# Accumulators put in banks one group ahead, residual rows loaded at once, first left-over rows split in place

## The chip, the cores and the metric

The kernel runs on one core of one Trainium2 chip. The metric is the device time of one execution in microseconds (us), the median over the runs. The engines are called PE (matrix multiplication, with PEld for its weight loads), DVE (vector), ACT (scalar), POOL and SP; SP does nothing but issue transfers (DMA), which ACT also issues. "Banks" are the eight banks of PSUM, the memory that PE writes its sums to.

## The reference

One transformer block on 2048 rows of 576 features, in fp32: an adaptive layer norm, a segmented linear-memory attention, a residual; then a second adaptive layer norm, a gated feed-forward layer with 4608 hidden features, and a residual.

```python
mod = (_silu(c) @ w_mod).reshape(c.shape[0], 6, 1, -1)
sa, ca, ga, sb, cb, gb = (mod[:, 0], mod[:, 1], mod[:, 2], mod[:, 3], mod[:, 4], mod[:, 5])
h = _layernorm(x) * (1 + ca) + sa
x = x + ga * _A_ref(h, A_wq, A_wk, A_wv, A_wo, A_beta)   # 32 heads, 4 segments of 512 rows, output times wo
h = _layernorm(x) * (1 + cb) + sb
x = x + gb * ((_silu(h @ w_gate) * (h @ w_up)) @ w_down)
```

## The kernel before, in words

**Precision.** Every fp32 operand is split into a high part (a cast to the PE's fp32r format, on ACT) and a low part (value minus high part, on DVE); a product is then three matmuls, high x high, high x low and low x high. Products of 2 x 2 blocks use a seven-product scheme, so operands are sums and differences of blocks as well.

**Up to 523 us.** Layer norm, q, k, v, attention and the output product wo run interleaved, in an order written out by hand. The last stage of it, wo for the last segment (`wo_m`, 32 small blocks n = 0 to 31, products at line 876), runs from 523 to 552 us. In its loop, work for the feed-forward half is placed at fixed n: loads of the operands `y` (`load_y`, four blocks of 1 MB and their remainder), three more operand blocks that are made in place (`y_here`), sums and splits of the first weights (`O` to `wh` and `wl`, `prep_w`).

**Left-over rows.** The 576 features are 4 x 128 + 64, so each seven-product has a seventh matmul over 96 rows, whose weights are three stacked copies (high, low, high) of 32 left-over rows, in two tiles `R` (`wr0`, `wr1`). Left-over rows of four weight blocks at a time come as a tile `RB` (`load_rb`), are summed (`sum_rb`), split (`split_rb`: `RH` on ACT, the low part on DVE), and stored to a DRAM buffer `rD` (`store_rb`), from where `prep_r` loads the wanted 32 rows three times. For the first two tiles `first_r` takes them from `RB` by six transfers on ACT's queue.

**The feed-forward half, from 552 us.** Loops over 2 halves of the tokens (t), 18 blocks of hidden features (p, "passes") and 14 steps (k). A step is one of the seven products of gate or up: seven matmuls of 512 columns at line 1459, into one of the banks A, B or C. ACT copies from these (`tb`, `tc`, B; line 1488 and 1505) feed the sums on DVE that make gate times up. Between the steps stands the down projection of the pass before: in passes 8 to 16 of the first half, 14 groups c = 0 to 13 of six matmuls of 288 columns (line 1589), one per step, two at steps 4 (c = 4 and 5) and 11 (c = 11 and 12), none at steps 6 and 13. The matmuls of a group write a tile `pd` of two banks, of which there are two. For nine of the 14 groups (`PA7`) the running sum `acc` is copied into the tile by ACT ahead of the matmuls (line 1569), and out of it behind them (line 1593); for the others DVE adds the tile to the sum (line 1597). `down` asks for its own and the next group's tile ahead of its matmuls, and for the one after that behind them (`ahead`). In the second half the sums are added on DVE alone. In passes 1 to 7 the down projection has another form (line 1613).

**Operand preparation for the second half.** `prep2` is a generator, advanced at steps of passes 1 to 7: it loads five blocks of 128 rows of the residual stream `xD`, normalises them (statistics on DVE at line 1300, scale on ACT), stores them, and then makes the operands of the second half from them. The rows go through two buffers.

**What sets the order.** Each engine works through its own instructions in the order of the program; waits are semaphores. A tile from a pool is written only when its last readers are done. Transfers use eight semaphores in turn, so a transfer also waits for the one that was issued eight before it. Low parts are put in a list `later` and issued with the next step.

Of the kernel before, what the change touches and what calls it, by code (L numbers as in the profile page):

```python
# [15 lines left out]
P = 128  # L16
S = 2048
D = 576
# [4 lines left out]
L = 512  # L23
# [78 lines left out]
def f32(ap):  # L102
    return ap.bitcast(F32)
# [3 lines left out]
def block(ctx: ExitStack, tc: tile.TileContext, x, wqk, wv, wo, beta, wgu, wrm, wd, c, w_mod, wm01, out):  # L107
# [1154 lines left out]
            later.append(lambda: nc.vector.tensor_tensor(d[64:96], f[64:96], f32(d[64:96]), op=ALU.subtract))  # L1262

    def prep2(x2p):
        ha = xp.tile([P, 2, L], F32, tag="xs", name="ha")
        xb = xp.tile([P, 4, 2, P], F32, tag="xs", name="xb")[:, :, 0]
        t3 = x2p.tile([P, 256], F32, tag="t3", name="t3")

        def opr(kb, hv, o, f):
# [11 lines left out]
            yield  # L1281

        xl2 = x2p.tile([P, D], F32, tag="xl2", name="xl2")
        xls = (ha.rearrange("p a b -> p (a b)")[:, :D], xl2)
        rows = ((2, 3), (3, 0), (3, 1), (3, 2), (3, 3))

        def load_row(j):
            sn, i = rows[j]
            nc.sync.dma_start(xls[j % 2], xD[sn][:, i, :])
        load_row(0)  # L1290
        load_row(1)
        for _ in range(5):
            yield
        for j, (sn, i) in enumerate(rows):
            xl = xls[j % 2]
# [12 lines left out]
            nc.scalar.activation(xl, xl, AF.Identity, scale=rs[:, 0:1], bias=nb[:, 0:1])  # L1308
            nc.sync.dma_start(xhD[sn][:, i, :], xl)
            if j < 3:  # L1310
                load_row(j + 2)
            yield
        xbs = (xb, xl2[:, :L].rearrange("p (a b) -> p a b", b=P))

# [70 lines left out]

    RB = {}

    def load_rb(j):
        RB[j] = opl.tile([P, 7, P], F32, tag="RB", name="RB")
        nc.sync.dma_start(RB[j][:, 0:4], wrm[j])  # L1390

    def sum_rb(j, i):
        sum_w(RB[j], i, nc.gpsimd if j else nc.vector)

    def split_rb(j):
        r = RB[j]
        rh = RB[j, 1] = opl.tile([P, 7, P], F32R, tag="RH", name="RH")
        nc.scalar.copy(rh, r)
        later.append(lambda: nc.vector.tensor_tensor(r.bitcast(F32R), r, f32(rh), op=ALU.subtract))

    def first_r():
        for z in range(2):
            for c in range(3):
                v = RB[0] if c == 1 else f32(RB[0, 1])
                nc.scalar.dma_start(f32(R[z][32 * c:32 * c + 32]), v[32 * z:32 * z + 32])

    def store_rb(j):
        lo, hi = RB.pop(j), f32(RB.pop((j, 1)))
        for c, v in ((0, hi), (2, hi), (1, lo)):
            nc.scalar.dma_start(rD[j][c], v)  # L1410

# [148 lines left out]
    PD = {}  # L1560
# [13 lines left out]
            down_new(t, *v)  # L1574

    def down(t, p, c):
        for j in range(c, c + 2 - t):
            ahead(t, p, j)
        m, q = POS[c // 2], c % 2
        ah, al = AP[p % 2, m]  # L1580
        dh, dl = DP[p % 2, m]
        pd = PD[t, p, c]
        new = p == (0 if t else P7) and m not in (2, 3, 4)
        on_act = t == 0 and c in PA7
        first = new or not on_act
        for i in range(2):
            tk = slice(128 * (2 * q + i), 128 * (2 * q + i) + 128)
            for k, (a, w) in enumerate(((ah, dh), (ah, dl), (al, dh))):
                nc.tensor.matmul(pd[:, i, :288], lhsT=a[:, tk], rhs=w, start=(first and k == 0), stop=(k == 2),  # L1589
                                 skip_group_check=not first)  # L1590
        o = down_acc(t, c)
        if on_act:
            nc.scalar.copy(o, pd[:, :, :288])  # L1593
        elif new:
            nc.vector.tensor_copy(o, pd[:, :, :288])
        else:
            nc.vector.tensor_tensor(o, o, pd[:, :, :288], op=ALU.add)  # L1597
        if t == 0:
            ahead(t, p, c + 2)

    def plain(t, p, c):
        end = t and p == NPR - 1 and c == 7
# [53 lines left out]
    with tc.manual_schedule():  # L1656
# [58 lines left out]
        ys = [hvp.tile([P, L], F32, tag="hh2", name="ys"), yt[2][:, 4, :L],  # L1715
              pool(p5, "ys").tile([P, L], F32, tag="ys", name="ys")]
        load_o(0, 0, 0)
        load_rb(0)
        for kb in range(3):
            y_sum(kb)  # L1720
        load_y(0, 0)
# [14 lines left out]
        for i in range(4):  # L1736
            for h in range(2):
                for c in range(WC):
                    n = 8 * i + 4 * h + c
                    wo_m(3, i, h, c)  # L1740
                    if c == 3:
                        wo_x(3, i, h)
                    flush()
                    if n in SS:
                        j = SS.index(n)
                        sum_o(0, j // 4, j % 4, nc.vector if j > 3 else nc.gpsimd)
                    if n == 6:
                        for z in range(2):
                            nc.gpsimd.memset(f32(R[z][96:128]), 0.0)
                        for o in ACT_OP.values():  # L1750
                            nc.gpsimd.memset(f32(y[96:128, o, 4]), 0.0)
                    if n == 9:
                        for j in range(4):
                            sum_rb(0, j)
                    elif n == 10:
                        split_rb(0)
                    elif n == 12:
                        first_r()
                    elif n == 28:
                        store_rb(0)  # L1760
                    if n == 24:
                        nc.scalar.activation(omg[:, 0:1], omg[:, 0:1], AF.Silu)
                        store_o(0, 0)
                    if n in HH:
                        y_here(HH.index(n))
                    if n in WW:
                        prep_w(0, 0, next(gw))
                if h == 1 and i < 2:
                    wo_r(3, i + 2)
                    wo_s(3, i + 2)  # L1770
                    wo_t(3, i + 2)
# [21 lines left out]
        for t in range(2):  # L1793
            for p in range(NPR):
# [17 lines left out]
                for k in range(14):  # L1812
# [28 lines left out]
                    else:  # L1841
# [158 lines left out]
```

## Time and profile before

| | us |
|---|---|
| median of 3 runs | 1808.68 (1804.61 to 1812.76) |
| the profiled execution | 1806.46 |
| its span | 1804.7 |
| PE busy | 1762.7 (98%) |
| PE loading weights | 1496.8 (83%) |
| DVE busy | 1473.2 (82%) |
| ACT busy | 1032.2 (57%) |
| POOL busy | 486.2 (27%) |
| last wo stage | 523 to 552 |
| first half of the feed-forward part | 552 to 1178 |
| second half | 1178 to the end |

In rows of the timeline the columns are the start (us), the duration (us), engine, line, operation, output and input tiles, count, and in brackets how long the engine was idle before and what ended that. In rows of groups the numbers behind the bar are busy time, mean ns of one, and the idle time before such instructions with its releaser. In rows of windows, the busy time of each engine stands with its number of instructions, then the granted clock of PE, the busy share of the DMA engines and what they moved in GB/s. Matmuls overlap: a row of 0.29 us is followed by the next after 0.13.

### The profile page before, as it was taken

What the parts mean: (1) busy time and instruction counts of PE and PEld (TensorE: products, weight loads), DVE (VectorE), ACT (ScalarE), POOL (GpSimd) and SP (SyncE); (2) the same over time, 40 slices, a digit from 0 to 9 for tenths busy, and PEclk for the clock granted to TensorE, in tenths of its full rate; (3) what the DMA queues carried; (4) which work ended last, traced back from release to release, by engine and by line L of the source; (5) the groups of instructions that cost most, each with busy time, mean ns of one, the idle gap of its engine ahead of it and who ended that gap; (6) DMA issues with size and microseconds to landing.
All of it is one profiled execution on the core that took longest, in us unless ns stands there. A gap on an engine that the chain in (4) does not pass through costs nothing.

```text
span 1804.7 us, 31494 instructions
## 1 busy us (share of the span) xinstructions
PE 1762.7 (98%) x10945; PEld 1496.8 (83%) x10945; DVE 1473.2 (82%) x3290; ACT 1032.2 (57%) x2221; POOL 486.2 (27%) x748
## 2 busy tenths in 40 slices
PE   8999999999988999999999999999999999999999
PEld 5888777767767888888888888888888888888888
DVE  7567589989966788987888888868888888898886
ACT  6343578778855455545787777444544544544542
POOL 2010146555670555453454444100000000000000
PEclk9999999999999999999999999999999999999999
DMA  8678765577668677644544544594324324324331
GB/s 310 224 234 278 239 200 175 169 198 210 192 216 303 202 240 231 208 153 134 175 137 136 182 141 137 172 302 150 102 85 131 106 81 130 108 80 131 108 104 53
DMA packets 149190, 309.85 MB, mean 172 GB/s; under 512 B 28184, under 2 KB 60376, under 8 KB 147240
## 3 DMA queue, kind: packets, MB, share of 16 engines
q1 hardware_dynamic: 134536, 253.29, 46.0%
q10 hardware_dynamic: 14496, 54.55, 7.7%
q8 instruction: 87, 1.43, 0.3%
q14 instruction: 71, 0.58, 0.1%
HBM read 193.04 MB, written 113.33 MB: 170 GB/s over the span
## 4 chain that ended last, share of the span: by engine, by line
PE 72%; DMA 4%; DVE 4%; ACT 4%; issue 1%; POOL 1%; ACTq 0%; SPq 0%; DVEq 0%; POOLq 0%
PE A L1459 22%; PE pd L1589 14%; PE C L1459 11%; PE pd L1613 6%; PE B L1459 6%; PE pw L876 3%; PE av L768 3%; PE s L713 2%; PE s L742 2%; PE pn L1012 1%; DVE junk L213 1%; ACT acc L1593 1%; DMA O<-in_wgu_dram 1%; DMA y<-yD 1%; DMA wd<-dr__15586 1%
## 5 line engine op out<-in xcount | busy, mean ns | idle before, releaser
L1459 PE MATMUL A<-y,wh 128*128 128x512 f32 x1152 | 404.3, 391 | 3.1 <-ACT tb L1488 2.0
L1459 PEld LDWEIGHTS A<-y,wh 128*128 128x128 f32 x1152 | 216.4, 188 | 43.7 <-ACT tb L1488 3.2
L1597 DVE TENSOR_TENSOR acc<-acc,pd 128x576 f32<-128x576 f32 x258 | 193.7, 751 | 64.6 <-PE pd L1589 58.9
L1424 DVE TENSOR_TENSOR wl<-O,wh 128x256 fp32r<-128x256 f32 x504 | 245.2, 490 | 1.4 <-ACT wh L1423 0.9
L213 DVE CUSTOM_DVE_ANT_0 junk<-s,tri 128x384 bf16<-128x384 f32 (+3 forms) x512 | 218.5, 486 | 22.7 <-PE s L713 8.9
L1459 PE MATMUL A<-y,wl 128*128 128x512 f32 x576 | 224.9, 390 | 0.0
L1589 PE MATMUL pd<-dh,ah 128*128 128x288 f32 x700 | 208.7, 298 | 8.8 <-ACT acc L1593 8.8
L1423 ACT CAST wh<-O 128x256 fp32r<-128x256 f32 x504 | 199.5, 406 | 17.8 <-DMA wr<-RH 9.4
L1589 PE MATMUL pd<-dl,ah 128*128 128x288 f32 x700 | 206.1, 294 | 0.0
L1589 PE MATMUL pd<-dh,al 128*128 128x288 f32 x700 | 205.1, 293 | 0.0
L1459 PE MATMUL C<-y,wh 128*128 128x512 f32 x576 | 202.7, 393 | 0.0
L1529 DVE TENSOR_TENSOR al<-sg,ah 128x512 fp32r<-128x512 f32 x219 | 160.9, 735 | 7.9 <-ACT ah L1528 7.3
L1528 ACT CAST ah<-sg 128x512 fp32r<-128x512 f32 x219 | 135.9, 621 | 52.0 <-DVE sg L1483 43.8
L1589 PEld LDWEIGHTS pd<-dh,ah 128*128 128x128 f32 x700 | 131.4, 188 | 22.5 <-ACT acc L1593 10.6
L1414 POOL TENSOR_TENSOR O<-O 128x256 f32<-128x256 f32 x132 | 114.6, 885 | 124.3 <-DMA O<-in_wgu_dram 57.4
L749 ACT ACTIVATE Pt<-s 128x512 f32<-128x512 f32 x256 | 135.4, 598 | 21.6 <-PE s L742 11.8
L1589 PEld LDWEIGHTS pd<-dl,ah 128*128 128x128 f32 x700 | 132.4, 189 | 13.1
L1589 PEld LDWEIGHTS pd<-dh,al 128*128 128x128 f32 x700 | 132.1, 189 | 0.0
L1459 PEld LDWEIGHTS C<-y,wh 128*128 128x128 f32 x576 | 108.0, 188 | 18.9
L1459 PEld LDWEIGHTS A<-y,wl 128*128 128x128 f32 x576 | 108.1, 188 | 15.4
L1459 PE MATMUL A<-y,wr 128*128 128x512 f32 x288 | 113.8, 395 | 0.0
L1459 PE MATMUL C<-y,wl 128*128 128x512 f32 x288 | 112.2, 389 | 0.0
(422 smaller groups left out, 4305.1 us busy)
## 6 DMA issues: line engine op xcount, KB each, us to landing
wr<-rD SPq DMA_DIRECT2D x207, 112.0 KB
O<-in_wgu_dram SPq DMA_DIRECT2D x36, 512.0 KB
O<-oD SPq DMA_DIRECT2D x36, 512.0 KB
oD<-O ACTq DMA_DIRECT2D x34, 512.0 KB
ks<-kD SPq DMA_DIRECT2D x64, 216.0 KB
qs<-qD SPq DMA_DIRECT2D x64, 216.0 KB
O<-in_wgu_dram SPq DMA_DIRECT2D x36, 384.0 KB
y<-yD SPq DMA_DIRECT2D x11, 1024.0 KB
```

Source lines behind the costliest of these rows:

```text
L213: nc.vector.tensor_tensor_reduce(junk[:, :n], bank[:, o:o + n], tri[:, L - n:], 1.0, -3e38, op0=ALU.add, op1=ALU.max, accum_out=mcol[u][0] ...
L749: nc.scalar.activation(pt[:, h], bank, AF.Exp, scale=SCALE)
L768: nc.tensor.matmul(av[u][32 * h:32 * h + 32, 128 * j:L], lhsT=vq[s][:, j, VW * hh:VW * hh + 32], rhs=pt[:, h, c:c + L - 128 * j], start=(j ...
L1414: eng.tensor_tensor(o[:, d], o[:, a], o[:, b], op=op)
L1423: nc.scalar.copy(wh, o)
L1424: later.append(lambda: nc.vector.tensor_tensor(wl, o, f32(wh), op=ALU.subtract))
L1459: nc.tensor.matmul(bank, lhsT=a, rhs=b, start=(first and n == 0), stop=(n == 6), skip_group_check=not first)
L1528: nc.scalar.copy(ah, src)
L1529: later.append(lambda: nc.vector.tensor_tensor(al, src, f32(ah), op=ALU.subtract))
L1589: nc.tensor.matmul(pd[:, i, :288], lhsT=a[:, tk], rhs=w, start=(first and k == 0), stop=(k == 2), skip_group_check=not first)
L1597: nc.vector.tensor_tensor(o, o, pd[:, :, :288], op=ALU.add)
L1613: nc.tensor.matmul(pd[:, i, :288], lhsT=a[:, tk], rhs=w, start=(k == 0), stop=(k == 5))
```

## The change

There are three parts.

1. `down` asks for its own tile ahead of its matmuls and for the next group's tile behind them, ahead of its own copy-out. Before, it was two groups ahead. Only the first half does so; in the second, `down` asks for its own alone, as before.
2. `prep2` loads all five rows at its start, into halves of two larger tiles and one tile of its own, and has one more turn before the first row is read.
3. The first left-over rows: `load_first` loads the 32 rows three times, straight to the partitions where they are wanted, by six transfers on SP; `sum_first` sums them on DVE, four instructions over 96 partitions and both tiles; `split_first` writes each `R` by one cast on ACT, and the low part in its middle 32 partitions on DVE. The rows of `RB[0]`, wanted from the second pass on, are loaded, summed (on POOL), split and stored in steps 0 to 6 of the first pass. High and low parts now share one tile.

```diff
 def prep2(x2p):
-    ha = xp.tile([P, 2, L], F32, tag="xs", name="ha")
-    xb = xp.tile([P, 4, 2, P], F32, tag="xs", name="xb")[:, :, 0]
+    xa, xc = [xp.tile([P, 4, 288], F32, tag="xs", name=f"x{n}").rearrange("p a b -> p (a b)") for n in "ac"]
+    ha = xa[:, :2 * L].rearrange("p (a b) -> p a b", a=2)
+    xb = xc[:, :L].rearrange("p (a b) -> p a b", b=P)
...
-    xls = (ha.rearrange("p a b -> p (a b)")[:, :D], xl2)
+    xls = (xl2, xc[:, :D], xc[:, D:], xa[:, :D], xa[:, D:])
     rows = ((2, 3), (3, 0), (3, 1), (3, 2), (3, 3))
-    def load_row(j):
-        sn, i = rows[j]
-        nc.sync.dma_start(xls[j % 2], xD[sn][:, i, :])
-    load_row(0)
-    load_row(1)
-    for _ in range(5):
+    for j, (sn, i) in enumerate(rows):
+        nc.sync.dma_start(xls[j], xD[sn][:, i, :])
+    for _ in range(6):
         yield
...
         nc.sync.dma_start(xhD[sn][:, i, :], xl)
-        if j < 3:
-            load_row(j + 2)
         yield
...
-def first_r():
+def load_first():
+    RB["first"] = r = new_rb()
     for z in range(2):
         for c in range(3):
-            v = RB[0] if c == 1 else f32(RB[0, 1])
-            nc.scalar.dma_start(f32(R[z][32 * c:32 * c + 32]), v[32 * z:32 * z + 32])
+            nc.sync.dma_start(r[32 * c:32 * c + 32, z, 0:4], wrm[0][32 * z:32 * z + 32])
+
+def sum_first(i):
+    sum_w(RB["first"][0:96].rearrange("p z a b -> p a z b"), i, nc.vector)
+
+def split_first(z):
+    r = RB["first"][:, z]
+    nc.scalar.copy(R[z][0:96], r[0:96])
+    later.append(lambda: nc.vector.tensor_tensor(R[z][32:64], r[32:64], f32(R[z][32:64]), op=ALU.subtract))
...
 def down(t, p, c):
-    for j in range(c, c + 2 - t):
-        ahead(t, p, j)
+    ahead(t, p, c)
...
+    if t == 0:
+        ahead(t, p, c + 1)
     o = down_acc(t, c)
     if on_act:
         nc.scalar.copy(o, pd[:, :, :288])
...
-    if t == 0:
-        ahead(t, p, c + 2)
...
-    load_rb(0)
+    load_first()
...
                 if n == 9:
                     for j in range(4):
-                        sum_rb(0, j)
-                elif n == 10:
-                    split_rb(0)
-                elif n == 12:
-                    first_r()
-                elif n == 28:
-                    store_rb(0)
+                        sum_first(j)
+                elif n in (11, 14):
+                    split_first(n // 14)
...
+                    elif p == 0 and k < 8:
+                        if k == 0:
+                            load_rb(0)
+                        elif k == 2:
+                            for j in range(4):
+                                sum_rb(0, j)
+                        elif k == 4:
+                            split_rb(0)
+                        elif k == 6:
+                            store_rb(0)
```

What follows are pieces of the engines' own orders. The lines of the changed kernel differ from those of before by a few (1569 is 1574, 1593 is 1599, 1423 is 1428, 1488 is 1493, 1379 is 1374, 1405 is gone).

ACT in the last wo stage, before (`hh` is the cast that the next wo products read, `wh` the high part of a weight block):

```order
L1398 CAST RH_8555<-RB_8436 128x896
L1423 CAST wh_8563<-O_8434 128x256
L1405 DMA wr0_8421<-RH_8555 32x896
L1405 DMA wr0_8421<-RB_8436 32x896
L1405 DMA wr0_8421<-RH_8555 32x896
L1405 DMA wr1_8422<-RH_8555 32x896
L1405 DMA wr1_8422<-RB_8436 32x896
L1405 DMA wr1_8422<-RH_8555 32x896
L1423 CAST wh_8590<-O_8434 128x256
L855 CAST hh_8598<-pto_8593 128x512
```

And now:

```order
L1409 CAST wr0_8421<-RB_8436 96x896
L1428 CAST wh_8566<-O_8434 128x256
L1409 CAST wr1_8422<-RB_8436 96x896
L1428 CAST wh_8590<-O_8434 128x256
L855 CAST hh_8598<-pto_8593 128x512
```

The six transfers ahead of `hh` are gone from ACT, and there are two casts where one was.

SP around the rows of `prep2` (in the first passes), before (`ha` and `xl2` are the two buffers, `xh` the normalised rows in DRAM):

```order
L1289 DMA ha_9000<-xD2_125 128x576
L1289 DMA xl2_9003<-xD3_126 128x576
L1373 DMA O_9019<-in_wgu_dram 128x1024
L1384 DMA wr1_8422<-rD0_181 32x896 x3
L1309 DMA xh2_121<-ha_9000 128x576
L1289 DMA ha_9000<-xD3_126 128x576
L1373 DMA O_9217<-in_wgu_dram 128x1024
L1309 DMA xh3_122<-xl2_9003 128x576
L1289 DMA xl2_9003<-xD3_126 128x576
L1384 DMA wr0_8421<-rD1_182 32x896 x3
L1309 DMA xh3_122<-ha_9000 128x576
L1289 DMA ha_9000<-xD3_126 128x576
```

And now:

```order
L1288 DMA xl2_9011<-xD2_125 128x576
L1288 DMA xc_9009<-xD3_126 128x576 x2
L1288 DMA xa_9008<-xD3_126 128x576 x2
L1368 DMA O_9030<-in_wgu_dram 128x1024
L1379 DMA wr1_8422<-rD0_181 32x896 x3
L1306 DMA xh2_121<-xl2_9011 128x576
L1368 DMA O_9226<-in_wgu_dram 128x1024
L1306 DMA xh3_122<-xc_9009 128x576
```

The three later loads no longer stand behind the stores of earlier rows; all five follow one another.

ACT at steps 10 to 12 of a pass of the first half, before (the tile `pd_12648` is that of group 12, `pd_12592` that of group 10; `tc` is the copy of the product of step 11):

```order
L1593 COPY acc7_11549<-pd_12592 128x576
L1569 COPY pd_12648<-acc3_8715 128x2x288
L1448 CAST dh_12650<-dr__12379 128x288
L1423 CAST wh_12653<-O_12404 128x256
L1488 COPY tc_12665<-A_12542 128x512
L1379 DMA oD10_0_165<-O_12404 128x1024
L1593 COPY acc3_8715<-pd_12648 128x576
```

And now:

```order
L1599 COPY acc7_11554<-pd_12622 128x576
L1453 CAST dh_12651<-dr__12381 128x288
L1428 CAST wh_12654<-O_12406 128x256
L1493 COPY tc_12666<-A_12543 128x512
L1374 DMA oD10_0_165<-O_12406 128x1024
L1574 COPY pd_12677<-acc3_8712 128x2x288
L1599 COPY acc3_8712<-pd_12677 128x576
```

The copy-in of group 12 moved from right behind the copy-out of group 10 to behind `tc` and a transfer, just ahead of its own matmuls.

More of the change, by code (lines that the diff above doesn't have):

```diff
@@ L1283, in prep2 @@
         xl2 = x2p.tile([P, D], F32, tag="xl2", name="xl2")
-        xls = (ha.rearrange("p a b -> p (a b)")[:, :D], xl2)
+        xls = (xl2, xc[:, :D], xc[:, D:], xa[:, :D], xa[:, D:])
         rows = ((2, 3), (3, 0), (3, 1), (3, 2), (3, 3))
-        def load_row(j):
-            sn, i = rows[j]
-            nc.sync.dma_start(xls[j % 2], xD[sn][:, i, :])
-        load_row(0)
-        load_row(1)
-        for _ in range(5):
+        for j, (sn, i) in enumerate(rows):
+            nc.sync.dma_start(xls[j], xD[sn][:, i, :])
+        for _ in range(6):
             yield
         for j, (sn, i) in enumerate(rows):
-            xl = xls[j % 2]
+            xl = xls[j]
             st = x2p.tile([P, 2, 6], F32, tag="st3", name="st3")
@@ L1386, in block, with new_rb @@
     RB = {}
+    def new_rb():
+        return opl.tile([P, 2, 7, P], F32, tag="RB", name="RB")
     def load_rb(j):
-        RB[j] = opl.tile([P, 7, P], F32, tag="RB", name="RB")
-        nc.sync.dma_start(RB[j][:, 0:4], wrm[j])
+        RB[j] = new_rb()
+        nc.sync.dma_start(RB[j][:, 0, 0:4], wrm[j])
     def sum_rb(j, i):
-        sum_w(RB[j], i, nc.gpsimd if j else nc.vector)
+        sum_w(RB[j][:, 0], i, nc.gpsimd)
     def split_rb(j):
-        r = RB[j]
-        rh = RB[j, 1] = opl.tile([P, 7, P], F32R, tag="RH", name="RH")
+        r, rh = RB[j][:, 0], RB[j][:, 1].bitcast(F32R)
         nc.scalar.copy(rh, r)
         later.append(lambda: nc.vector.tensor_tensor(r.bitcast(F32R), r, f32(rh), op=ALU.subtract))
-    def first_r():
+    def load_first():
+        RB["first"] = r = new_rb()
         for z in range(2):
             for c in range(3):
-                v = RB[0] if c == 1 else f32(RB[0, 1])
-                nc.scalar.dma_start(f32(R[z][32 * c:32 * c + 32]), v[32 * z:32 * z + 32])
+                nc.sync.dma_start(r[32 * c:32 * c + 32, z, 0:4], wrm[0][32 * z:32 * z + 32])
[5 more added lines that the diff above has]
+        later.append(lambda: nc.vector.tensor_tensor(R[z][32:64], r[32:64], f32(R[z][32:64]), op=ALU.subtract))
     def store_rb(j):
-        lo, hi = RB.pop(j), f32(RB.pop((j, 1)))
+        lo, hi = [RB[j][:, i] for i in range(2)]
         for c, v in ((0, hi), (2, hi), (1, lo)):
@@ L1581, in down @@
         dh, dl = DP[p % 2, m]
-        pd = PD[t, p, c]
+        pd = PD.pop((t, p, c))
         new = p == (0 if t else P7) and m not in (2, 3, 4)
```

## The prediction

> **What bounds the kernel now.** I read the first part of the page, then the groups, then the windows of the feed-forward half, and last the rows of single engines at the holes of PE. An execution like the profiled one takes 1806.46 us, 1804.7 of them span.
>
> ```profile
> span 1804.7 us, 31494 instructions
> PE 1762.7 (98%) x10945; PEld 1496.8 (83%) x10945; DVE 1473.2 (82%) x3290; ACT 1032.2 (57%) x2221; POOL 486.2 (27%) x748
> ...
> L1589 PE MATMUL pd<-dh,ah 128*128 128x288 f32 x700 | 208.7, 298 | 8.8 <-ACT acc L1593 8.8
> ...
> L1423 ACT CAST wh<-O 128x256 fp32r<-128x256 f32 x504 | 199.5, 406 | 17.8 <-DMA wr<-RH 9.4
> ```
>
> PE is the bound: it is idle for 42 us of the span. Only two things can move the time, then: holes of PE that close or open, and time in which PE is busy but slow. The groups name a hole of 8.8 before the down projection and a wait of ACT, 9.4, for a small transfer. The windows show the holes by stage.
>
> ```profile
> core 0: us, PE busy (x) PEld busy (x) DVE busy (x) ACT busy (x) POOL busy (x), PEclk, DMA share, GB/s
> ...
> 523.00:538.00 15.00, 13.87 (x104) 13.12 (x102) 10.32 (x18) 5.03 (x9) 12.30 (x17) 1.00 1.03 338
> 538.00:547.00 9.00, 0.20 (x2) 0.15 (x1) 2.26 (x6) 3.17 (x7) 0.00 (x0) 0.61 0.97 276
> 547.00:552.20 5.20, 5.20 (x29) 5.20 (x30) 3.60 (x9) 1.68 (x4) 0.00 (x0) 0.69 0.99 369
> 552.20:575.00 22.80, 22.80 (x103) 18.90 (x102) 18.27 (x41) 14.82 (x35) 0.58 (x1) 1.00 0.80 275
> ...
> 600.00:625.00 25.00, 22.75 (x111) 19.14 (x110) 17.75 (x37) 10.70 (x23) 10.22 (x14) 0.93 0.72 222
> ...
> 875.00:910.00 35.00, 33.59 (x182) 29.32 (x181) 30.41 (x46) 26.85 (x58) 15.40 (x16) 1.00 0.51 165
> ```
>
> From 538 to 547 PE works 0.20 us, in 600 to 625 it lacks 2.25, and in a pass of the first token half (875 to 910) 1.41. Each part of the change aims at one of these.
>
> **First left-over rows: 7.5 us gained.** Six transfers of split rows into R leave ACT's queue. What they cost shows in the rows of ACT, and then of DVE and PE.
>
> ```profile
> 533.13 0.94 ACT L1398 CAST RH<-RB 128x896 fp32r<-128x896 f32 x1 [3.39 <-DVE RB L1414]
> ...
> 534.11 0.60 ACTq L1405 DMA_DIRECT2D wr<-RH  x1
> ...
> 543.26 0.51 ACTq L1405 DMA_DIRECT2D wr<-RH  x1
> 543.82 0.40 ACT L1423 CAST wh<-O 128x256 fp32r<-128x256 f32 x1 [9.44 <-DMA wr<-RH]
> 544.13 0.58 ACT L855 CAST hh<-pto 128x512 fp32r<-128x512 f32 x1
> ```
> ```profile
> 534.11 1.09 DVE L1399 TENSOR_TENSOR RB<-RB,RH 128x896 fp32r<-128x896 f32 x1 [0.64 <-ACT RH L1398]
> ...
> 544.74 0.69 DVE L859 TENSOR_TENSOR hl<-pto,hh 128x512 fp32r<-128x512 f32 x1 [8.84 <-ACT hh L855]
> ```
> ```profile
> 546.88 0.58 PE L876 MATMUL pw<-woh,hh 128*128 128x288 f32 x1 [8.80 <-DVE xr L881]
> ...
> 550.33 0.29 PE L876 MATMUL pw<-woh,hh 128*128 128x288 f32 x1
> ```
>
> A cast that PE's last wo blocks need (hh) stands behind the sixth transfer, which could be issued only at 543.26. PE stops 8.80 before 546.88, at 538.08. Without the transfers ACT runs, from 533.13 on, two casts of 96x896 in place of one of 128x896 (0.94 each, by its row) and two wh (0.40 each), 2.7 us, so hh may begin at 535.8. From there on the order is that of before, in which 544.13 to 546.88, 2.75 us, pass between hh and PE: PE could go on at 538.6, 0.5 after it stopped. DVE has more to do ahead of hl: sums of twice the elements, and two subtractions of 32x896, which I price at 1.09 each, the row of 128x896; one of them is extra. I let 0.8 of that show. PE also stops running slowly: between 546.88 and 550.33 stand 14 matmuls, which at the pitch of 0.134 that the rows after 550.33 have would take 1.9 us and took 3.45, so 1.5 are lost to the granted clock (0.61 and 0.69 in the windows). The gain is 8.80 − 0.5 − 0.8 + 1.5 = 9.0; bounds: none, if another wait holds the hole open, and 10.3, if nothing of it stays.
>
> The loads of y might be such a wait.
>
> ```profile
> y<-yD SPq DMA_DIRECT2D x4, 1024.0 KB
> ...
> y<-yD SPq DMA_DIRECT2D x4, 192.0 KB
> ```
>
> By the windows, 5.1 MB moved from 523 to 538 (15.0 x 338) and 2.5 more until 547. The four blocks of y are 5.0 MB, and what is loaded ahead of the last of them (four rows of x, two weight tiles, the left-over rows) is 2.6, together 7.6, so the last block would lie there near 547. The first product that reads it is the fifth, four steps after the start (7 matmuls of 0.23, 1.6 us each): 543.2 + 6.4 = 549.6. So it covers, by some 2.5 us.
>
> The other work on these rows moves into the first pass: the load of 256 KB, four sums on POOL, a cast and a subtraction, and three stores.
>
> ```profile
> 574.42 2.68 POOL L1414 TENSOR_TENSOR RB<-RB 128x128 f32<-128x128 f32 x4 [36.71 <-DMA RB<-in_wrm_dram]
> ...
> 567.47 1.21 SPq L1390 DMA_DIRECT2D RB<-in_wrm_dram  x1
> ```
>
> The next such load took from 567.47 to 574.42, 7 us, and its four sums 2.68. From the load (k=0) to the cast on ACT (k=4) the first pass has about 6 us; load and sums need 9.7. The cast then blocks ACT's queue for up to 4 us, with copies of PE's banks behind it; ACT has slack (14.82 of 22.80 busy in this window), and the cast of 0.94 itself lies in it. Bounds: 0 and 4; I take 1.5, since a late copy of one bank leaves PE the steps on the two others, about 3 us. Left: 9.0 − 1.5 = 7.5.
>
> **Rows of the operand preparation: 3.9 us gained.** Before, five row loads share two buffers, and a load waits for the store of an earlier row from the same buffer. Below, what DVE's statistics of these rows (L1300) waited for, and rows of SP, ACT and PE.
>
> ```profile
>   DMA ha<-xD: 8.5, 3
> ```
> ```profile
> 603.06 0.42 SPq L1309 DMA_DIRECT2D xh<-ha  x1
> 606.55 0.34 SPq L1289 DMA_DIRECT2D ha<-xD  x1
> ```
> ```profile
> 616.93 0.59 ACT L1488 COPY tb<-A 128x512 f32<-128x512 f32 x1 [3.73 <-DVE cu L1482]
> ```
> ```profile
> 617.57 0.50 PE L1459 MATMUL A<-y,wh 128*128 128x512 f32 x1 [2.01 <-ACT tb L1488]
> ...
> 618.13 0.72 PE L1459 MATMUL A<-y,wh 128*128 128x512 f32 x2
> ...
> 622.03 0.29 PE L1613 MATMUL pd<-dh,ah 128*128 128x288 f32 x1
> ```
>
> The last load is issued at 606.55, after the store at 603.06, and its DVE statistics hold up DVE's queue (8.5 us in three such waits); DVE is then late with cu, ACT with tb, PE by 2.01. Between 618.13 and 622.03 stand 5 gate/up matmuls (0.23 each at full pitch) and 9 of the down projection (0.133): 2.35, and it took 3.9. So 2.0 + 0.24 for a smaller hole before it + 1.55 slow + 0.1 restart = 3.9. Loaded at once, the rows lie there before they are read, with a DMA share of 0.7 to 0.8 in these windows. Nothing is added but one idle turn of the generator, half a step. Bounds: 0, if DVE is late here for its own work, and 5, if smaller lags go too.
>
> [...]
>
> **Accumulators one group ahead: 4.8 us gained.** In nine passes (8 to 16) the down projection runs in 14 groups per pass, the sums of nine being copied into a bank before their group and out after it, on ACT. At steps 4 and 11 two groups stand together.
>
> ```profile
> 874.90 0.29 PE L1589 MATMUL pd<-dh,al 128*128 128x288 f32 x1
> 876.61 0.40 PE L1589 MATMUL pd<-dh,ah 128*128 128x288 f32 x1 [1.41 <-ACT acc L1593]
> ```
> ```profile
> 911.26 0.40 PE L1589 MATMUL pd<-dh,ah 128*128 128x288 f32 x1 [0.79 <-ACT acc L1593]
> ```
>
> Group 5 waits for the copy-out of group 4, whose bank it shares. At the pitch of 0.13 it was due at 875.03 and began at 876.61; with 0.1 of restart (0.40 where the others have 0.29) that is 1.68, 0.27 more than its idleness. At 911.26 it is 0.79 + 0.27 = 1.06. Each comes four times (the group row counts 8.8 us of idleness): 4 x 1.68 + 4 x 1.06 = 11.0; by the group row, 8.8 + 8 x 0.27 = 10.9. With one group ahead, two banks alternate strictly, so group 5 waits only for group 3, long done.
>
> What is added is at group 12, the second of the pair at step 11. Its copy-in now stands behind that step's copy tc.
>
> ```profile
> 892.51 0.40 PE L1459 MATMUL A<-y,wr 128*128 128x512 f32 x1
> ...
> 893.55 0.29 PE L1589 MATMUL pd<-dh,ah 128*128 128x288 f32 x1
> ```
> ```profile
> 893.13 0.59 ACT L1488 COPY tc<-A 128x512 f32<-128x512 f32 x1
> ```
> The product's last matmul starts at 892.51 and ends near 892.94. tc starts there at the earliest and occupies ACT for some 0.48 (its 0.59 overlaps the next), the copy-in 0.65 (0.64 in the row below): 894.07, and PE follows at 894.13. Group 12 was due at 893.55: 0.58 late, with restart 0.68, in nine passes 6.1. If tc came as late as in the row (893.13), 0.87 a pass. Behind PE nothing else is queued but the next products. Against that, a wait goes:
>
> ```profile
> 899.46 0.64 ACT L1569 COPY pd<-acc 128x576 f32<-128x576 f32 x1 [2.50 <-DVE acc L1597]
> ```
>
> ACT idled 2.50 us a pass for DVE with a copy-in that was early; PE did not wait for it, so this is worth nothing by itself, but it gives ACT room. The copy-ins of groups 1, 4, 6 and 8 end 0.3 to 0.6 ahead of their matmuls in my replay of ACT's order with these durations. Net 10.9 − 6.1 = 4.8; bounds: −5 (group 1 late too, below) and 10.9 (group 12 on time).
>
> **The sum.** 1806.46 − 7.5 − 3.9 − 4.8 = 1790.3. The median of the runs before, 1808.68, lies 2.2 above the profiled execution; I forecast **1791** as the median.
>
> **Rivals.** (1) DMA and the first pass take back the first part: y late, or ACT held the full 4 us and more by the cast. For it: shares of 0.97 to 1.03, and 7 us for one load. Against: the bytes counted above, and PE's other banks. With 0 in place of 7.5 the time is 1797.8, so 1798.
>
> (2) The banks bring nothing: group 1's copy-in also comes late, by the dh and ah casts ahead of it on ACT (0.43 and 0.62 at 895.70 and 896.03 in the pass before).
>
> ```profile
> 895.70 0.43 ACT L1448 CAST dh<-dr__12379 128x288 fp32r<-128x288 f32 x1
> 896.03 0.63 ACT L1528 CAST ah<-sg 128x512 fp32r<-128x512 f32 x1
> ```
>
> Then 9 x (0.68 + 1.05) = 15.6 stands against 10.9, and the time is 1790.3 + 9.5 = 1799.8. For it: the margin of 0.3. Against: the 2.50 us that ACT gains.
>
> (3) Slower: ACT lags in the whole first half of each pass, because a copy-in, now one group ahead, is no longer started early enough to absorb a late cast. Groups 1 to 4 each lose x us in nine passes: 36x. From x = 0.45 the kernel is not faster than before, from 0.70 slower by over 0.5%, and with a full 1.0 it takes 1826. For it: ACT is busy 26.85 of 35 there. Against: that leaves 8 us a pass, about 0.55 in each step of a product and a group (2.4 us), so a late copy catches up within two steps.
>
> (4) The change does not shorten the preparation: DVE, 18 of 25 us busy, is late at 616 for its own queue. The 3.9 stay away: 1794.
>
> **Chances.** My forecast 0.55, (1) 0.14, (2) 0.12, (4) 0.12, (3) 0.07. About 0.5%, 9 us, is what a measurement of this kernel tells from no change: faster means under 1799.6, slower over 1817.7. The forecast and (4) count as faster nearly whole, (1) in two of three cases, (2) in half: 0.77 faster. Slower is most of (3), 0.05; the rest, 0.18, is the same. The forecast's own range, from the bounds 10.3 and 5 and a free group 12 down to a first pass stalled by 4 us, is 1781 to 1796; with (1), (4) and (2) the range is 1781 to 1803.
>
> **What would show it.** Right: no ACT idleness on transfers near 535 to 544 and the feed-forward half starting 8 to 10 us earlier; no hole of PE near 617 less the shift; no wait of PE on a copy-out at step 4, but one of about 0.6 on a copy-in at step 11, in nine passes, each 34.3 long. Wrong: holes of PE in the first pass on ACT's copies, waits on copy-ins at groups 1 to 4, or the hole at 538 still there with another releaser, a load of y.

## The result and the profile after

The changed kernel takes 1798.19 us (median; 1796.27 to 1799.2), the kernel before 1808.67 in the same comparison: a ratio of 0.9942, with a 95% interval of 0.9924 to 0.9961. It is faster, by 10.5 us; 1791 was forecast. Measured again later, beside 16 runs of the kernel before with a median of 1804.65, it took 1799.33, a ratio of 0.9967 (0.9955 to 0.9979), 5.3 us by the medians and 6.0 by the ratio. The medians of the changed kernel agree; those of the kernel before differ by 4 us. The gain is therefore some 5 to 10 us, about a third to two thirds of the 16.2 us of the prediction's sum; the two intervals together reach from 4 to 14.

The page of the changed kernel, its first lines and those groups that answer to the ones shown of before:

```profile
span 1794.6 us, 31522 instructions
PE 1762.9 (98%) x10945; PEld 1494.9 (83%) x10945; DVE 1470.0 (82%) x3292; ACT 1036.7 (58%) x2223; POOL 486.8 (27%) x752
...
L1464 PE MATMUL A<-y,wh 128*128 128x512 f32 x1152 | 404.5, 392 | 4.3 <-ACT tc L1493 4.0
...
L1593 PE MATMUL pd<-dh,ah 128*128 128x288 f32 x700 | 209.2, 299 | 5.2 <-ACT pd L1574 5.2
...
L1428 ACT CAST wh<-O 128x256 fp32r<-128x256 f32 x504 | 199.6, 406 | 4.8 <-issue 3.2
```

ACT's wait of 9.4 for a transfer is gone, and so is the hole of 8.8 before the down projection. Two new waits stand in their place: 5.2 on a copy-in (L1574), and 4.0 on a copy `tc` before a gate/up product. To see where they lie I divided both executions at the same places of the program: the wo stage from the end of its first longer hole (0.93 us in both) to the first gate/up product, then the first, second and third pass (numbers 0, 1 and 2), then the passes numbered 8 to 16 together. The first number behind the window is its length. Before:

```profile
522.79:552.20 29.41, 19.48 (x133) 18.68 (x134) 16.40 (x31) 9.87 (x19) 12.51 (x17) 0.83 1.00 325
552.20:572.82 20.62, 20.62 (x93) 17.07 (x92) 16.13 (x36) 13.61 (x32) 0.00 (x0) 1.00 0.77 263
572.82:608.51 35.69, 35.60 (x195) 30.95 (x194) 27.32 (x58) 16.67 (x36) 20.01 (x26) 1.00 0.80 279
608.51:648.89 40.38, 38.13 (x203) 33.14 (x202) 26.38 (x47) 18.55 (x42) 19.64 (x25) 0.96 0.62 190
829.46:1142.80 313.34, 304.56 (x1639) 266.07 (x1638) 265.74 (x409) 236.91 (x501) 137.33 (x138) 1.00 0.46 149
```

After:

```profile
521.53:542.92 21.39, 17.94 (x133) 17.15 (x133) 18.56 (x32) 11.46 (x22) 12.66 (x17) 1.00 1.01 326
542.92:569.61 26.69, 22.68 (x93) 18.07 (x92) 17.22 (x37) 13.57 (x31) 1.73 (x4) 0.94 0.86 293
569.61:605.65 36.04, 35.66 (x195) 30.97 (x194) 27.88 (x58) 16.88 (x36) 18.55 (x26) 1.00 0.80 284
605.65:642.17 36.52, 36.28 (x203) 31.88 (x202) 25.80 (x48) 18.58 (x41) 19.34 (x25) 1.00 0.63 198
822.00:1133.62 311.62, 306.38 (x1640) 266.02 (x1638) 266.95 (x409) 238.97 (x501) 138.03 (x138) 1.00 0.47 150
```

| stretch | change, us | in the prediction |
|---|---|---|
| everything up to the end of that first hole (not touched) | −1.3 | 0 |
| wo stage | −8.0 | −9.0 |
| first pass | +6.1 | +1.5 |
| second pass | +0.4 | 0 |
| third pass | −3.9 | −3.9 |
| passes 3 to 7 | −0.7 | 0 |
| passes 8 to 16 | −1.7 | −4.8 |
| the pass that begins the second half (wait for a load of y, there or not from execution to execution) | −1.0 | 0 |
| all | −10.1 | −16.2 |

So the wo stage and the third pass came as worked out, and two terms were too good: the first pass, which gave back 6.1 of the 8.0 us just won, and the passes with the accumulators. The first row of the table and the last but one are no effect of the change: over all profiled executions of this case that hole ended between 521.4 and 525.7 us, whatever the kernel, and the wait for y appears in some of them and not in others.

**The first pass.** Rows of SP, POOL, ACT and PE of the changed kernel:

```profile
544.02 1.67 SPq L1436 DMA_DIRECT2D dr__8715<-in_wd_dram  x2
547.73 0.33 SPq L1388 DMA_DIRECT2D RB<-in_wrm_dram  x1
...
553.16 1.80 POOL L1419 TENSOR_TENSOR RB<-RB 128x128 f32<-128x128 f32 x4 [15.87 <-issue]
...
554.99 0.94 ACT L1395 CAST RB<-RB 128x896 fp32r<-128x896 f32 x1 [6.08 <-POOL RB L1419]
555.84 0.40 ACT L1428 CAST wh<-O 128x256 fp32r<-128x256 f32 x1
556.14 0.58 ACT L1493 COPY tc<-A 128x512 f32<-128x512 f32 x1
...
556.77 0.62 PE L1464 MATMUL A<-y,wh 128*128 128x512 f32 x1 [4.01 <-ACT tc L1493]
557.19 0.63 PE L1464 MATMUL A<-y,wl 128*128 128x512 f32 x1
```

Read downward, it is one chain. The load of `RB` leaves SP at 547.73, 4.8 us into the pass; POOL's sums start 5.4 us later, once the load has landed (at 552.86; the row names no releaser); the cast on ACT waits for them, 6.08 us idle, with `tc` behind it; and PE waits 4.01 for `tc`, after which it runs at half pitch (0.42 from row to row, where the rows of the steps before have 0.23). Two weight loads stand ahead of the load on SP, but what held it last shows in SP's waits between 543 and 549 (us in total, times, the longest):

```profile
SPq L1388 <- DMA y<-yD: 2.0, 1, 2.0
```

The transfer issued eight before this one was the last block of y, 1 MB; it left SP at 533.83 and landed at 547.66, 0.07 us ahead of the load of `RB`.

**Passes 8 to 16.** The row of PE at step 11 and the two of ACT that set it, then the same for group 8 of an odd pass:

```profile
885.24 0.59 ACT L1493 COPY tc<-A 128x512 f32<-128x512 f32 x1 [0.28 <-PE A L1464]
...
885.72 0.65 ACT L1574 COPY pd<-acc 128x576 f32<-128x576 f32 x1
...
886.42 0.40 PE L1593 MATMUL pd<-dh,ah 128*128 128x288 f32 x1 [0.42 <-ACT pd L1574]
```
```profile
873.82 0.81 ACTq L1415 DMA_DIRECT2D rD<-RB  x2
...
874.67 0.64 ACTq L1415 DMA_DIRECT2D rD<-RB  x1
875.35 0.71 ACT L1428 CAST wh<-O 128x256 fp32r<-128x256 f32 x2 [0.42 <-issue]
...
877.00 0.63 ACT L1574 COPY pd<-acc 128x576 f32<-128x576 f32 x1
...
877.69 0.40 PE L1593 MATMUL pd<-dh,ah 128*128 128x288 f32 x1 [0.35 <-ACT pd L1574]
```

The 0.42 at group 12, with 0.27 of restart 0.69, is the 0.68 of the prediction. The 0.35 at group 8, 0.62 with restart, was not in it: in odd passes ACT issues three stores of left-over rows in step 6, and what is queued behind them, the copy-in of group 8 last, comes late.

### The profile page after: what moved, and what is told of

It reads as the page before. It is cut to its first block, busy times and chain, and to the rows that moved or that the text cites. A ratio compares the mean times of both kernels' runs of the same rounds, so it can differ in the third digit from the quotient of the medians.

```text
span 1794.6 us, 31522 instructions
## 1 busy us (share of the span) xinstructions
PE 1762.9 (98%) x10945; PEld 1494.9 (83%) x10945; DVE 1470.0 (82%) x3292; ACT 1036.7 (58%) x2223; POOL 486.8 (27%) x752
## 4 chain that ended last, share of the span: by engine, by line
PE 74%; DVE 4%; DMA 3%; issue 2%; ACT 2%; POOL 2%; ACTq 0%; SPq 0%; DVEq 0%; POOLq 0%
PE A L1464 23%; PE pd L1593 14%; PE C L1464 12%; PE pd L1617 8%; PE B L1464 6%; PE av L768 3%; PE pw L876 2%; PE s L742 2%; PE s L713 2%; PE pn L1012 1%; DMA O<-in_wgu_dram 1%; DVE wl L1429 1%; PE pw L953 1%; DVE junk L213 1%; DVE sg L1540 1%
## 5 line engine op out<-in xcount | busy, mean ns | idle before, releaser
L1603 DVE TENSOR_TENSOR acc<-acc,pd 128x576 f32<-128x576 f32 x258 | 193.6, 751 | 71.4 <-PE pd L1593 66.7
L1627 DVE TENSOR_TENSOR acc<-acc,pd 128x576 f32<-128x576 f32 x84 | 63.0, 750 | 61.8 <-PE pd L1617 61.7
```

## Experiments

Two theories were set against each other. Mine, from the traces: each of the three parts does what it says, and the missing 6 to 10 us are two orders on queues, the load of `RB[0]` late on SP (first pass) and the copy-in of group 12 behind `tc` on ACT. The rival: the transfers as a whole (share 1.0 until 552, 0.8 after) and ACT's lack of room set these stretches, so that a wait taken away comes back elsewhere.

**The accumulators: taken out, put in alone, and mended.** First, the changed kernel with the old `down`:

```diff
 def down(t, p, c):
-    ahead(t, p, c)
+    for j in range(c, c + 2 - t):
+        ahead(t, p, j)
...
-    pd = PD.pop((t, p, c))
+    pd = PD[t, p, c]
...
-    if t == 0:
-        ahead(t, p, c + 1)
     o = down_acc(t, c)
...
+    if t == 0:
+        ahead(t, p, c + 2)
```

> The changed kernel (1798.2 us) with the old form of `down`, two groups ahead. By the two traces passes 8 to 16 together became 1.7 us shorter by the new form, so this should take 1799.9, with odd passes of 35.27 and even ones of 34.65 and the 1.41 and 0.79 us holes back at group 5. By the sum of the prediction (4.8 for this part) it would take 1803.0.

It took 1799.06 us, 0.9969 of before (0.9957 to 0.9981), not to be told from the changed kernel by the time, and its passes 8 to 16 together 313.49 against 311.62. The holes at group 5 are back:

```profile
L1594 PE MATMUL pd<-dh,ah 128*128 128x288 f32 x700 | 208.7, 298 | 8.7 <-ACT acc L1598 8.7
```

The kernel before with nothing but the new `down`:

> The kernel before with only the new form of `down`. By the pass lengths in the traces (holes of 1.68 and 1.06 at group 5 gone, 0.69 at group 12 and 0.62 at group 8 of odd passes come) it brings 1.7 us, a ratio of 0.999; by the sum of the prediction 4.8, 0.9973.

1802.0 us, 0.999 (0.9979 to 1.0), passes 8 to 16 in 311.06. By the lengths of these passes, this part as it stands is worth about 2 us, both ways; the times alone do not show it.

Then the changed kernel with one copy-in placed elsewhere:

```diff
+    if t == 0 and prev is not None and not is_plain(*prev) and k in {11: 12}:
+        ahead(*prev, {11: 12}[k])
     if k != 1 or prev is not None:
         step(z, m)
```

> The changed kernel, with the copy-in of group 12 issued ahead of step 11, so that it stands on ACT ahead of the copy tc. Theory: the 0.42 us hole (0.69 with restart) at group 12 is the price of that place in ACT's order and goes in nine passes: 1798.2 - 6.2 = 1792.0, even passes 33.65, odd ones 34.27. Rival: ACT has no room there and the lateness moves to tc, so that PE waits for the copy of bank A instead: 1797 to 1799.

1790.12 us, 0.9919 (0.9906 to 0.9932). Passes 8 to 16 are without a hole:

```profile
823.69:1126.81 303.12, 303.12 (x1639) 265.44 (x1638) 267.68 (x409) 238.32 (x501) 139.43 (x138) 1.00 0.49 155
```

PE is busy for the whole window. The gain, 311.62 − 303.12 = 8.5, is more than the 6.2 expected: the lateness at group 8 of odd passes shrank too (these passes took 33.74 to 33.80, the even ones 33.61), though its order was not touched. ACT had the room; the rival falls for this stretch.

**The first pass: the load earlier.**

```diff
+    elif n == 17:                # in the loop of the wo stage
+        load_rb(0)
...
-    if k == 0:
-        load_rb(0)
-    elif k == 2:
+    if k == 2:
```

> The changed kernel, with the load of RB[0] issued in the wo stage (n = 17, between the second and third store of xD) and no longer in step 0 of the first pass, where it left SP at 547.73; sums, cast and stores stay. Theory: the late load holds POOL's sums, these hold ACT's cast, this holds tc and PE (4.0 us and 2 us at half clock in the first pass): the first pass goes from 26.7 back to 20.7 and the time to 1792.2. Rival: the transfers as a whole are what is full until 552 (share 1.0), so an earlier load only pushes others back (y, weights) and PE stands elsewhere in the first pass: 1796 to 1799.

1794.9 us, 0.9945 (0.9929 to 0.996): between the 1792.2 of the theory and the 1796 to 1799 of the rival, and its interval overlaps those of the changed kernel as it was (0.9942 and 0.9967). The first pass fell from 26.7 to 22.9 us, and the second rose from 36.0 to 39.8:

```profile
545.65:568.59 22.94, 21.26 (x93) 16.93 (x92) 17.13 (x37) 13.49 (x31) 1.76 (x4) 1.00 0.91 314
568.59:608.40 39.81, 36.88 (x196) 32.34 (x194) 27.84 (x58) 17.09 (x36) 18.31 (x26) 0.96 0.76 275
```
```profile
588.95 0.50 PE L1464 MATMUL A<-y,wr 128*128 128x512 f32 x1 [2.93 <-DMA wr<-rD]
```

What was gained in the first pass was lost to the load of the second tile of left-over rows for the second pass, which reads what the first pass stored and stands on SP behind the five row loads of the preparation. So the late load did hold up ACT and PE (its hole went from 4.01 to 1.24), and that was not the last limit. Nor did the earlier place help by its full length: the load left SP 7.2 us earlier in the pass (543.25, 2.4 us ahead of its start), but POOL's sums began only 2.2 us earlier (553.70, 8.05 into the pass and not 10.24), for now 10.5 us lie between the load and the sums, where there were 5.4. So much of the rival holds in the first pass too.

All three edits of this kind together, the copy-in of group 8 ahead of step 7 being the third:

```diff
+    if t == 0 and prev is not None and not is_plain(*prev) and k in {11: 12, 7: 8}:
+        ahead(*prev, {11: 12, 7: 8}[k])
     if k != 1 or prev is not None:
         step(z, m)
```

> The edits of the two runs before together, and the copy-in of group 8 issued ahead of step 7 (in odd passes it stands behind three stores and two copies on ACT and PE waits 0.35 us, 0.62 with restart, in four passes). If the three causes are separate: 1798.2 - 6.2 - 6.0 - 2.5 = 1783.5, with passes 9 to 16 all near 33.65. If ACT is short of room, the gains of the copy-ins are given back at tc or B: 1788 to 1792.

1786.93 us, 0.9898 (0.9885 to 0.9911). That lies between the two forecasts. The copy-ins brought all that was asked of them: passes 8 to 16 are 33.61 each, 9.2 us less than in the changed kernel. The earlier load did not: the first pass took 21.7 and the second 38.9, with the same hole, now 2.00, together 2.2 us less in place of 6.0.

**The second pass: what stands ahead of the load.** Two edits of that kernel. In the first, `prep_r` for the second tile was called in step 0 of the second pass and not in step 2:

```diff
-    if k == 2 and p:
+    if p and k == (0 if p == 1 else 2):
         prep_r(0, p, 1)
```

> The kernel of the last run (three edits, 1786.9) with the load of the second tile R for the second pass issued in its step 0, ahead of the five row loads of the preparation on SP, and not in step 2 behind them. There PE waits 2.0 us for it at 587 and is slow after. Theory: its place behind 1.4 MB of rows is the cause; the hole and the slow clock go and the second pass takes 36.0 in place of 38.9: 1784.1. Rival: the volume of the transfers sets these passes; then another transfer comes late by as much: 1786 to 1787.

1795.3 us, 0.995 (0.9938 to 0.9962), a second pass of 48.4. It was a bad edit: the product of step 1 still belongs to the first pass and reads that tile, so here it was computed with the second pass's rows, and had to wait for them:

```profile
568.74 1.76 SPq L1379 DMA_DIRECT2D wr<-rD  x3
```
```profile
579.12 0.77 PE L1464 MATMUL C<-y,wr 128*128 128x512 f32 x1 [11.13 <-DMA wr<-rD]
```

Its use is the price it shows: three transfers of 112 KB, issued between 568.7 and 570.5 with the row loads behind them and not ahead, were there only at 579 (DMA share 1.05 and 335 GB/s from 565 to 579).

The second edit spreads the five loads of the preparation:

```diff
-    for j, (sn, i) in enumerate(rows):
+    def load_row(j):
+        sn, i = rows[j]
         nc.sync.dma_start(xls[j], xD[sn][:, i, :])
-    for _ in range(6):
+    load_row(0)
+    load_row(1)
+    for j in range(6):
         yield
+        if j in (3, 4, 5):
+            load_row(j - 1)
```

> The same kernel with the five row loads spread: two at the start, the third in the fourth turn and two more in the two turns after it, so that 0.6 MB stands ahead of the load of R and not 1.4. Theory: 0.9 MB less at about 300 GB/s is 2.9 us, the hole at 587 goes, 1784.1, and no later hole appears, since the rows are read one after another. Rival: as above 1786 to 1787; or a row comes late to DVE and a part of the old hole in the third pass comes back: 1787 to 1791.

1786.13 us, 0.9902 (0.9889 to 0.9915), by the interval the same as without it. In its profiled execution the hole is 0.65 us and the second pass 35.9, as the theory had it:

```profile
567.49:603.40 35.91, 35.26 (x195) 31.02 (x194) 27.19 (x58) 16.88 (x36) 18.43 (x26) 1.00 0.86 300
```

With the load of R in step 1, its earliest place, in addition (`if p and k == (1 if p == 1 else 2):`):

> The kernel with the spread row loads, and in the second pass the load of the second R in step 1 (behind the last product that reads the old rows) and not in step 2, so ahead of the two weight and two row loads on SP. If its place on SP sets the last hole of the second pass (0.65 us at 585.6), it goes, with restart about 1 us: ratio 0.9895 to 0.990. If the volume of the transfers does, a hole of that size stays in this pass: 0.990 to 0.991.

1786.84 us, 0.9899 (0.9885 to 0.9912), and a second pass of 39.6, since another transfer was late:

```profile
585.77 0.61 PE L1622 MATMUL pd<-dh,ah 128*128 128x288 f32 x1 [2.80 <-DVE acc L1632]
```

Here the chain runs back from DVE's sum through its statistics of a row to that row's load (7.6 us from release to landing) and to a load of residuals (10.5 us). From the first gate/up product to the end of the second pass it was 56.3 us before, 62.7 in the changed kernel, 62.8 with the earlier load, 60.5 with the three edits, 58.2 with the loads spread and 62.3 here. For the second pass the rival is not refuted: the holes move among the transfers, and three orders of them give medians within 0.8 us, though the one trace of each differs by up to 4 us in these two passes. That the volume is the cause is not shown either, since nothing that lessens it was tried.

**The other two parts taken out.** The changed kernel with the old row loads (the second part of the change reversed):

> The changed kernel (1798.2 us) with the old row loads of `prep2`, two buffers and a load behind each store. Theory: the hole of PE in the third pass and the slow matmuls behind it come back, 3.9 us: 1802, with a third pass of 40.4 in place of 36.5. Rival 1: the slowness had another cause than the hole, then 2.3: 1800.5. Rival 2: DVE was late for its own queue, or the loads land in time now that the third pass begins earlier: 1798, with a third pass of 36.5.

1799.92 us, 0.9975 (0.9966 to 0.9985). The hole is back, but what follows it runs at full pitch:

```profile
617.33 0.50 PE L1469 MATMUL A<-y,wh 128*128 128x512 f32 x1 [2.01 <-ACT tb L1498]
617.66 0.39 PE L1469 MATMUL A<-y,wl 128*128 128x512 f32 x1
...
619.05 0.29 PE L1622 MATMUL pd<-dh,ah 128*128 128x288 f32 x1
619.19 0.29 PE L1622 MATMUL pd<-dl,ah 128*128 128x288 f32 x1
```

The third pass took 38.87, 2.35 more than with the new loads: rival 1's number, though not by another cause than the hole (last section). Beside the changed kernel measured again (0.9967) the difference is within the intervals.

And with the old handling of the first left-over rows (the third part reversed):

> The changed kernel with the old handling of the first left-over rows (six transfers on ACT, the load, split and store of RB[0] in the wo stage). From the two traces: the feed-forward half would start 8.0 us later, and the first two passes would take 56.3 in place of 62.7, so this part is worth 1.6: 1799.8. By the sum of the prediction (7.5 for this part) it would take 1805.7.

1798.99 us, 0.997 (0.9958 to 0.9981), the same as the changed kernel measured again. The hole of 9.12 and the half clock after it are back, and the first pass is short:

```profile
525.70:555.71 30.01, 19.71 (x132) 18.92 (x133) 16.43 (x31) 10.80 (x21) 12.48 (x17) 0.83 0.99 323
555.71:576.38 20.67, 20.67 (x94) 17.09 (x92) 16.13 (x36) 12.68 (x30) 0.00 (x0) 1.00 0.77 259
```

From the hole at 525.70 to the end of the second pass it is 86.5 us here and 84.1 (605.65 − 521.53) in the changed kernel: this part, which removes a hole of 9 us, is worth 2.4 by these two traces. Over all traces without another edit to the left-over rows it is 85.5 to 86.5 with the old handling and 84.1 to 85.3 with the new, so it may be less.

**The changed kernel again.**

> The changed kernel once more, beside the next two runs on the same chip, since the medians of the kernel before differed by some 4 us between chips. Expected 0.994 of before, as measured; if the removal of the new `down` (0.9969 in its run) really cost only 1.7 us, the ratio here must be nearer 0.996.

1799.33 us, 0.9967 (0.9955 to 0.9979). With this base the removal of the new `down` (0.9969) and its addition alone (0.999) do not contradict each other: both put this part at 0 to 2 us, within the intervals.

## Why the prediction was right, and where it was not

*Direction and range.* Faster was right, and 1798.19 lies in the range of 1781 to 1803; it lies 7 us above the forecast. A sign that the prediction itself gave for being wrong appeared: a hole of PE in the first pass on a copy of ACT. The first part kept 1.9 us of its 7.5, for the reason of rival (1), ACT held for more than 4 us. That the time also meets that rival's 1798 is partly luck: the accumulators brought 3.1 less than the sum had, and 2.3 us came from stretches that the change does not touch. Two small slips are in the sum: with the 2.2 by which the prediction has the median above the profiled execution, 1790.3 gives 1792.5 and not 1791; and the top of its own range, with a first pass stalled by 4 us, is 1791 + 2.5 = 1793.5 and not 1796.

*First left-over rows, the wo stage (9.0).* Measured 8.0: the hole of 8.80 became three of 1.97, 0.37 and 1.10 us where before had 0.86 and 0.27 besides, and the half clock went (the granted clock of the stage is 1.00 where it was 0.83). The sums of twice the elements cost DVE 2.92 us, against 2.40 for the old ones. The last block of y came just in time, and not 2.5 us early: it landed at 547.66, and the product that reads it, the fourth and not the fifth, began at 547.71. In variants PE waited up to 0.45 us for it.

*First left-over rows, the first pass (1.5, bounds 0 and 4).* This is the step that failed: "I take 1.5, since a late copy of one bank leaves PE the steps on the two others, about 3 us". Measured 6.1, outside the bounds. The load itself took 5.4 us, less than the 7 that I took, but was issued 4.8 us into the pass, when the block of y that was issued eight transfers before it had landed; I had it issued at step 0. ACT was then held 6.08 us. And this hole of 4 us cost more than its length, since the half clock behind it (0.50 for 3.41 us from 557.00 on) and the restart took about 2 us more (the pass is 6.07 us longer than before); I had counted that price for the holes that go and not for the one that comes. The experiments add that an earlier place helps by a part of its length only, since 10.5 us and not 5.4 then pass between the load and the sums, and that in the traces most of what it brings is lost in the second pass.

*Rows of the operand preparation (3.9).* The third pass fell by 3.9. But 1.6 of this was the half clock behind the old hole (0.50 for 3.41 us from 618.53 on), and this was not its regular price: with the old loads in the changed kernel the hole was again 2.01 us and the granted clock stayed at 1.00 in the whole pass, and in the kernel before with the new `down` alone the hole was 1.18. So this part is worth 1.5 to 3.9 us in the third pass, from one execution to the next, and 0.4 to 0.8 in passes 3 to 7, which take 179.83 us in all ten traces with the new loads and 180.2 to 180.6 in the three with the old. The price of a hole was taken from one profile.

*Accumulators (4.8).* Measured 1.7 from the traces and 0.999 alone. The 10.9 gained at group 5 and the 0.69 lost at group 12 in nine passes came as worked out. Missing was group 8 in odd passes, four times 0.62 us; its margin stood in the prediction (0.3 to 0.6 us "in my replay"), but without the three stores that ACT issues in step 6, which idle it for 0.42 us (issue). Without rounding, 10.9 − 6.1 − 2.5 = 2.3, and small lags make up the rest. Rival (2) had the right kind of fault (a copy-in that eats the gain) at the wrong group.

*Rivals (3) and (4)* did not occur: no copy-in of groups 1 to 4 came late, and each part did what it says.

## What to carry to other kernels

When work is moved from a stage with a hole into the next one, price there the whole chain that it brings, from the moment at which its first transfer can leave the queue, not only its busy time: here a load that had to wait until 1 MB issued eight transfers earlier had landed held POOL, ACT and PE in turn, and 6 of 8 us were gone. An order on a queue can be worth more than the change that it came with: one copy issued ahead of a step and not behind it, on an engine that is busy 77% of that stretch, made these passes 8.5 us shorter. The kernel with the new `down`, the copy-ins of groups 8 and 12 ahead of their steps and the earlier load takes 0.990 of the kernel before (1786 to 1787 us), less than either kernel of this case.

## What the runs showed of the hardware that was not expected

Holes of PE of the same length were not always followed by the half clock, a granted clock of 0.50 in the windows. Of those near 2 us, 2.01 at 617.57 in the kernel before and 2.00 at 587.20 in the variant with three edits were (matmuls of 288 columns at a pitch of 0.24), and 2.01 at 617.33 with the old row loads and 1.97 at 533.46 in the changed kernel were not:

```profile
533.46 0.37 PE L876 MATMUL pw<-woh,hh 128*128 128x288 f32 x1 [1.97 <-DVE xr L881]
533.67 0.29 PE L876 MATMUL pw<-wol,hh 128*128 128x288 f32 x1
533.80 0.29 PE L876 MATMUL pw<-woh,hh 128*128 128x288 f32 x1
```

Two holes of 2.19 us at the same matmul went one each way: in the run without the new `down` (533.90) the slow pitch of 0.24 came after the third matmul, in the run with the earlier load (536.19) the next six matmuls stood 0.13 apart. Of the longer holes, those of 2.80 (R in step 1), 2.93 (earlier load), 4.01 (changed kernel), 8.80 (before), 9.12 (old handling of the first left-over rows) and 11.13 us (R in step 0) were followed by it, at once or, behind the one of 2.93, 1.3 us later. Behind those of 1.41 us in passes 8 to 16 of the kernel before it did not come: the granted clock is 1.00 from 829.46 to 1142.80.

The windows show where the half clock begins and ends. First the interval with most of the hole at 617.57 in the kernel before and the interval behind it, then the same for the hole at 617.33 with the old row loads (PE's busy time stands behind the length, the granted clock is the third number from the end):

```profile
615.12:618.53 3.41, 1.40 (x6) 0.85 (x6) 3.38 (x7) 0.90 (x2) 2.44 (x2) 1.00 0.09 36
618.53:621.95 3.42, 3.42 (x13) 3.03 (x13) 1.44 (x3) 3.42 (x9) 0.00 (x0) 0.50 0.71 181
```
```profile
613.77:617.19 3.42, 1.54 (x7) 0.94 (x5) 3.28 (x8) 0.51 (x1) 2.83 (x3) 1.00 0.30 115
617.19:620.60 3.41, 3.27 (x19) 2.97 (x20) 2.64 (x5) 2.60 (x7) 0.31 (x1) 1.00 0.34 70
```

Between 100 and 1775 us the granted clock of the kernel before is 0.50 from 540.02 on for 10.24 us and from 618.53 on for 3.41, that of the changed kernel from 557.00 on for 3.41, and 1.00 elsewhere. The two beginnings in the first of these traces lie 78.51 us apart, 23 times 3.413, and 10.24 is three times that. If both traces are divided into windows of this length from these places, the hole at 617.57 lies whole in one, and the one of 1.97 at 533.46 in the changed kernel is split into 1.62 and 0.35; the two windows above split the hole at 617.33 into 1.87 and 0.14. In the windows just ahead of the three beginnings PE idled 1.94, 2.01 and 3.18 us (from 536.61, 615.12 and 553.59 on), and in no other window between 100 and 1775 us that had the full clock more than 1.62. That is a count from these two traces, not a rule for others. So the same hole in the third pass cost 3.86 us in one trace and 2.35 in another (40.38 and 38.87 beside 36.52); that its place among such windows decides which of the two is an estimate of mine from these rows; no run tests it.
